# A depthwise dynamic convolution with routed experts: spread scoring, paired moves, and stores of 128 partitions

## The chip, the cores and the metric

The kernel runs on one core of a Trainium2 chip. The metric is the device time of one execution in microseconds; before the change it was measured three times. A core has five engines that run at once and wait for each other by semaphores: TensorE (PE in the profile; PEld is its weight load), VectorE (DVE), ScalarE (ACT), GpSimd (POOL) and SyncE (SP), which here only issues transfers. Sixteen DMA engines move data between HBM and the on-chip memory SBUF. Matmul results land in PSUM.

## The reference

Input x is 8 batches of 4,160 tokens with 192 channels. Each token has for each of 8 heads 7 weights, which go through a softmax over the 7 taps; the output of the first part is a causal convolution with these weights. The second part scores every token of that output, takes the best 128 of each batch, sends them through two layers of 1,024 hidden units, and adds the gated result.

```python
w = exp(weight_gen - max(weight_gen, -1)); w = w / (sum(w, -1) + 1e-9)     # [8, 4160, 8, 7]
x_pad = concatenate([zeros((8, 6, 192)), x], axis=1)
y[b, s, h] = sum over k of w[b, s, h, k] * x_pad[b, s + k, h]              # 24 channels per head
scores = y @ w_gate                                                        # [8, 4160]
for b in range(8):
    top = the 128 tokens of highest score
    ye = maximum(y[b, top] @ w1, 0) @ w2                                   # 192 -> 1024 -> 192
    out[b, top] = y[b, top] + sigmoid(scores[b, top])[:, None] * ye        # other rows: out = y
```

## The kernel before

The 33,280 tokens are cut into 128 runs of 260 consecutive tokens (SP = 260); partition p holds run p. The main loop takes 65 steps (NSUB) of C = 4 tokens on all partitions, and has one more round for the lag of the last step. The order of the instructions on each engine is the order in which the Python code issues them; there is no scheduler behind it. Each round g does the following, with the sums and the store one step behind the products.

- `products(g)` (L770): VectorE multiplies a sliding window of x (fp16, in the ring `xr` of 168 tokens) by the doubled weights `wd`, for 7 taps x 4 tokens x 192 channels. The result is a `prod` buffer, one of three. While no list of selected rows exists it is one instruction; afterwards it is two, of taps 0 to 3 and 4 to 6 (L783).
- `tap_sums(prod, cps, half)` (L789): TensorE adds up the taps by matmuls with blocks of a 64 x 64 identity, into the PSUM tile `cps`, one of two. The two halves of a round (`half` 0 and 1) take taps 0 to 3 and 4 to 6. Partition 64 j + p of `cps` holds, at index i, half j of the four tokens' channels (HB = 384 values) of run 64 i + p.
- `store(g, cps)` (L801): ScalarE copies `cps` into `co`, one of three fp32 buffers (`outp`), and SyncE issues two transfers, one for each j: 64 partitions, each with two rows of 384 values.

Beside that, generators are moved on by `advance` in each half: `sm` (softmax weights of later steps, L657), `dt` (dot products with the gate vector: transposes of x on TensorE, L712, evicted by ScalarE, L716, then small matmuls, L697; 50 groups), `sc` (scores, from weights and dot products, L720) and `sel`. How many `dt` moves a half gets is set by DOTS: 0.82 per half, so 1.64 per round. DOTS also sets the rounds in which the loads of tokens 168 to 259 are issued (`late`, L863).

`sel` begins when all scores exist. First comes `threshold_selection` (L435): five rounds of top-8 lists of each partition, four rounds of a search for the threshold with a matmul each, then a matmul chain of 40 that makes the list of rows. It takes nine moves, one per round. Then comes `expert_pass` (L202), which gathers the selected rows and their weights by indirect transfers of GpSimd, convolves them anew, and runs the experts' layers; it gets two moves per round. Its table `steps` (L397) says at which move after its start each of a batch's ten operations comes; a new batch begins every third move (EVERY). At the end `scatter_rows` (L411) writes the rows of the 8 batches over those of the convolution, by indirect transfers that wait for all stores.

Of the kernel before, what the change touches and what calls it, by code (L numbers as in the profile page):

```python
# [9 lines left out]
FP16 = mybir.dt.float16  # L10
# [10 lines left out]
def kernel(  # L21
# [10 lines left out]
    nc = tc.nc  # L32
    B, S, D = x.shape
    H, K = weight_gen.shape[2], weight_gen.shape[3]
# [4 lines left out]
    P = 128  # L39
    N = B * S  # L40
    SP = N // P
# [4 lines left out]
    C = 4  # L46
    NSUB = SP // C
    BIG = 58
    CH = C * H
    HB = C * D // 2  # L50
# [7 lines left out]
    MUL, ADD = ALU.mult, ALU.add  # L58
# [3 lines left out]
    out_flat = out.rearrange("b s d -> (b s) d")  # L62
# [139 lines left out]
    def expert_pass(rowf, gates, result, big):  # L202
# [3 lines left out]
            out=rown[:, :], in0=rowf, scalar1=float(N - 1), scalar2=0.0,  # L206
# [6 lines left out]
            out=wst[:, :], in0=rown[:, :], scalar1=float(-PAD), scalar2=0.0,  # L213
# [4 lines left out]
            out=win_i[:, :], in0=wst[:, :], scalar1=float(D), scalar2=None, op0=MUL,  # L218
# [3 lines left out]
            out=head[:, :], in0=rown[:, 0:1], scalar1=float(PAD), scalar2=1.0e6,  # L222
# [4 lines left out]
            out=head_i[:, :], in0=rown[:, 0:1], scalar=float(D), op0=MUL,  # L227
            in1=head[:, :], op1=ADD,
# [3 lines left out]
            out=pos[:, :], in0=rown[:, :], in1=boff[:, :], op=ALU.subtract  # L232
# [3 lines left out]
            out=posk[:, :, :], in0=pos[:, :, None].to_broadcast([P, B, K]),  # L236
            in1=koff[:, None, :].to_broadcast([P, B, K]), op=ADD,
# [3 lines left out]
            out=inside[:, :, :], in0=posk[:, :, :], scalar1=float(PAD), scalar2=None,  # L241
# [113 lines left out]
        def hidden(b, half):  # L355
            if half == 0:
                hTs[b] = moep.tile([P, FC, P], BF16, tag="hT", name="hT")
            hps = ps2.tile([P, FC // 2, P], FP32, tag="tps", name="hps")
            for j in range(FC // 2):
                f0 = (half * (FC // 2) + j) * P  # L360
                nc.tensor.matmul(  # L361
                    out=hps[:, j, :], lhsT=w1_a[:, f0:f0 + P], rhs=xeTs[b][:, 0, :],
                    start=True, stop=False,
                )
                nc.tensor.matmul(  # L365
                    out=hps[:, j, :], lhsT=w1_b[:, f0:f0 + P], rhs=xeTs[b][:, 1, :],
                    start=False, stop=True,
                )
            nc.scalar.activation(  # L369
                out=hTs[b][:, half * (FC // 2):(half + 1) * (FC // 2), :],  # L370
                in_=hps[:, :, :], func=AF.Relu,
            )
# [19 lines left out]
        def hand_over(b):  # L392
# [2 lines left out]
            result["ready"].append(b)  # L395

        steps = {  # L397
            0: row_weights, 2: scale_weights, 4: double, 6: tap_rows, 8: conv_rows,
            9: turn_rows, 10: lambda b: hidden(b, 0), 11: lambda b: hidden(b, 1),
            13: outputs, 14: hand_over,  # L400
        }
        for _ in range(GWAIT):
            yield
        for t in range(EVERY * (B - 1) + 15):
            for off in sorted(steps, reverse=True):
                b, rem = divmod(t - off, EVERY)
                if rem == 0 and 0 <= b < B:
                    steps[off](b)
            yield
# [23 lines left out]
    fast = {}  # L433
# [150 lines left out]
    def phase():  # L584
# [6 lines left out]
        prodp = cctx.enter_context(tc.tile_pool(name="prodp", bufs=3))  # L591
# [165 lines left out]
        state = {"scored": 0, "weights": 0, "exps": 0}  # L757
        wds = {}
# [8 lines left out]
            for j in range(b - a):  # L767
                wds[a + j] = wd[:, j]

        def products(s):  # L770
            o = s * C % RING
            wd = wds.pop(s)
            prod = prodp.tile([P, K, C, D], FP16, tag="prod", name="prod")
            xwin = bass.AP(
                tensor=xr.tensor, offset=xr[:, o:o + 1, 0:1].offset,
                ap=[list(xr[:, :, :].ap[0]), [D, K], [D, C], [G, H], [2, G // 2], [1, 2]],
            )
            pv = prod.rearrange("p k t (h a b) -> p k t h a b", h=H, b=2)
            wv = (
                wd.rearrange("p k (c h) b -> p k c h b", h=H)[:, :, :, :, None, :]  # L780
                .to_broadcast([P, K, C, H, G // 2, 2])
            )
            for k0, k1 in ((0, 4), (4, K)) if "rowf" in fast else ((0, K),):  # L783
                nc.vector.tensor_tensor(  # L784
                    out=pv[:, k0:k1], in0=xwin[:, k0:k1], in1=wv[:, k0:k1], op=MUL
                )
            return prod

        def tap_sums(prod, cps, half):  # L789
            pf = prod.rearrange("p k t d -> p k (t d)")  # L790
# [10 lines left out]
        def store(s, cps):  # L801
            co = outp.tile([P, 2, HB], FP32, tag="co", name="co")
            nc.scalar.copy(out=co[:, :, :], in_=cps[:, :, 0:HB])  # L803
            for j in range(2):
                nc.sync.dma_start(
                    out=bass.AP(
                        tensor=out_flat.tensor, offset=out_flat.offset + s * C * D + j * HB,
                        ap=[[SP * D, 64], [64 * SP * D, 2], [1, HB]],
                    ),
                    in_=co[64 * j:64 * j + 64, :, :],  # L810
                )

        def selected():
# [13 lines left out]
        for p0, p1 in ((1, Q), (Q, P)):  # L827
            nc.sync.dma_start(
                out=halo[p0:p1, :],
                in_=bass.AP(  # L830
                    tensor=x_flat.tensor, offset=x_flat.offset + (SP * p0 - PAD) * D,
                    ap=[[SP * D, p1 - p0], [1, PAD * D]],
                ),
# [10 lines left out]
            out=start_p[:, :], in_=identity.rearrange("p (b q) -> p b q", q=Q)[:, :, 0],  # L844
# [3 lines left out]
            out=keep_p[:, :], in0=start_p[:, :], scalar1=-1.0, scalar2=1.0, op0=MUL, op1=ADD  # L848
        )
        for n in range(2):  # L850
# [4 lines left out]
            if n == 0:  # L855
                nc.vector.tensor_scalar(
                    out=xflat[:, 0:PAD * D], in0=halo[:, :],
# [6 lines left out]
        for a in range(RING, SP, 20):  # L864
            b = min(SP, a + 20)
            free = (b - RING + PAD - 1) // C + 1
            late.append((max(free, int((a + PAD) / (2 * DOTS * RUN * GRP / D)) - 4), a, b))
        dt, sc, sel = dots(), score(), None
        dup_at = {a - 2: n for n, (a, b) in enumerate(pieces) if n > 1}

        def advance(gen):
            next(gen, None)

        prods = {}
        done_dots, groups = 0.0, 0
        for g in range(NSUB + 1):
            if g < NSUB:
                prods[g] = products(g)
            for half in range(2):
                if g < 2 or (half == 0 and state["exps"] <= max(g + 8, groups * 4 / 3 + 14)):  # L880
                    advance(sm)
                if g >= 1:
                    done_dots += DOTS
                    if done_dots >= 1:
                        done_dots -= 1
                        groups += 1
                        advance(dt)
                advance(sc)
                if sel is None:
                    if state["scored"] == NSUB and half == 0:  # L890
                        sel = selected()
                elif half == 1 or "rowf" in fast:
                    advance(sel)
                if half == 0:
                    if g in dup_at:
                        dup_weights(dup_at[g])
                    if g == RING // C - 10:
                        nc.scalar.copy(out=xr[:, 0:PAD, :], in_=xr[:, RING:RING + PAD, :])
                if g > 0:
                    if half == 0:  # L900
                        cps = ps_c.tile([P, 2, 512], FP32, tag="cps", name="cps")
                    tap_sums(prods[g - 1], cps, half)
            if g > 0:
                store(g - 1, cps)
            if late and g >= late[0][0]:
                load_x(*late.pop(0)[1:])
            if g == 5:
                selection_masks()
            if g == 10:
                selection_constants()  # L910
            if g == 34:
                expert_weights()
            if LOG:
                print(g, state, "rowf" in fast, "complete" in fast)
# [4 lines left out]
    LOG = False  # L919
    GWAIT = 4  # L920
    EVERY = 3
    DOTS = 0.82
    with ExitStack() as cctx:
        with tc.manual_schedule():
            phase()
    flag_v = nc.values_load(fast["flag"][0:1, 0:1], min_val=0, max_val=2 * P * B)
    with tc.If(flag_v > 0):
        with ExitStack() as fctx:
# [5 lines left out]
            for _ in expert_pass(fast["rowf"][:, :], zero, undo, big):  # L934
                pass
# [5 lines left out]
                out=sv[:, :],  # L941
                in_=bass.AP(tensor=s_d.tensor, offset=s_d[:, :].offset, ap=[[S, B], [1, S]]),
# [3 lines left out]
            for i in range(CAP // 8):  # L946
# [4 lines left out]
                    out=sv[:, :], in_to_replace=top_v[:, sl], in_values=sv[:, :],  # L951
# [10 lines left out]
                out=sc_t[:, :], in_=bass.AP(tensor=v_d.tensor, offset=v_d[:, :].offset, ap=swap)  # L962
            )
            nc.sync.dma_start(
                out=ix_t[:, :], in_=bass.AP(tensor=i_d.tensor, offset=i_d[:, :].offset, ap=swap)
# [4 lines left out]
                out=row_g[:, :], in0=row_g[:, :], in1=boff[:, :], op=ADD  # L970
            )
            for _ in expert_pass(row_g[:, :], gate_values(sc_t[:, :]), redo, big):
                pass
# [36 lines left out]
```

## Time and profile before

| | |
|---|---|
| time, median of three | 321.94 us (320.14 to 322.54) |
| span of the profiled execution | 319.0 us |
| busy: TensorE / VectorE / ScalarE / GpSimd | 198.0 / 249.3 / 188.5 / 70.5 us |
| stores of the output | 130, of 192 KB each |
| HBM read and written | 41.60 and 26.35 MB |

The page divides the span into 40 slices of 8 us. Each digit is the busy share of an engine in tenths; the last two rows are the granted TensorE clock in tenths of full speed and the mean busy share of the sixteen DMA engines.

```
PE   0287298759688495999646414456617788799100
DVE  3786676988876396999999999999979988897000
ACT  4699579998955799699643203123305576766100
PEclk9999769986969788799989555556765979999755
DMA  6979999899999789946646302312739976355420
```

Read by columns: up to slice 19 (150 us) scoring and softmax run beside the convolution, and all engines and the DMA engines are busy. In slices 19 to 27 VectorE alone is full, with the threshold search. From slice 30 the experts run. In the last two or three slices the rows are scattered. A busy share is an average over its slice and does not say which engine others wait for; that takes the lists of waits and the chain.

### The profile page before, as it was taken

How to read it: one execution, taken by the hardware profiler on the slowest of the kernel's cores; microseconds unless marked ns; L12 is line 12 of the kernel's file. 1: busy time of each engine (PE TensorE's matmuls, PEld its weight loads, DVE VectorE, ACT ScalarE, POOL GpSimd, SP SyncE). 2: the span in 40 equal slices, each digit the busy share in tenths (PEclk: the TensorE clock that was granted, in tenths of full speed). 3: DMA queues.
4: the chain of work that ended last, by engine and by line, in shares of the span. 5: the costliest groups of instructions: out<-in, count | busy, mean ns of one | idle time of the engine just before them, and what ended most of it. 6: DMA issues, size and time to landing. Idle time of an engine off the chain costs nothing.

```text
span 319.0 us, 7498 instructions
## 1 busy us (share of the span) xinstructions
PE 198.0 (62%) x3177; PEld 124.3 (39%) x3177; DVE 249.3 (78%) x248; ACT 188.5 (59%) x282; POOL 70.5 (22%) x94
## 2 busy tenths in 40 slices
PE   0287298759688495999646414456617788799100
PEld 0155165536455263666323201114304455566000
DVE  3786676988876396999999999999979988897000
ACT  4699579998955799699643203123305576766100
POOL 2891020130120004000000000002388760000180
PEclk9999769986969788799989555556765979999755
DMA  6979999899999789946646302312739976355420
GB/s 162 301 173 249 296 235 222 184 240 254 273 234 241 261 161 215 208 117 150 170 128 150 95 7 59 89 49 63 185 60 163 203 179 148 78 120 129 106 84 16
DMA packets 28080, 51.48 MB, mean 161 GB/s; under 512 B 4805, under 2 KB 22219, under 8 KB 28042
## 3 DMA queue, kind: packets, MB, share of 16 engines
q1 hardware_dynamic: 21962, 33.62, 35.8%
q0 software_dynamic: 6080, 17.34, 30.8%
q8 instruction: 26, 0.43, 0.5%
q14 instruction: 12, 0.10, 0.1%
HBM read 41.60 MB, written 26.35 MB: 213 GB/s over the span
## 4 chain that ended last, share of the span: by engine, by line
PE 28%; ACT 23%; DVE 21%; DMA 13%; issue 8%; POOL 3%; SPq 1%; POOLq 0%; ACTq 0%; DVEq 0%
DVE prod L784 13%; PE cps L795 13%; DMA out_dram<-co 10%; ACT e L635 6%; ACT co L803 5%; ACT xT L716 4%; PE tps L712 4%; ACT wd L763 3%; POOL out_dram L417 2%; PE den L189 2%; PE yps L697 2%; PE yep L377 2%; DMA wg_t<-in_weight_gen_dram 2%; PE aps L335 1%; PE hps L361 1%
## 5 line engine op out<-in xcount | busy, mean ns | idle before, releaser
L784 DVE TENSOR_TENSOR prod<-xr,wd 128x5376 f16<-128x5376 f16 (+1 forms) x83 | 192.4, 2345 | 10.9 <-PE cps L795 5.4
L795 PE MATMUL cps<-prod,ident 64*64 64x384 f16 x1820 | 117.0, 386 | 26.7 <-DVE prod L784 22.9
L803 ACT COPY co<-cps 128x768 f32<-128x768 f32 x65 | 52.9, 814 | 63.2 <-PE cps L795 43.9
L795 PEld LDWEIGHTS <-ident 64*64 64x64 f16 x1820 | 49.8, 121 | 74.8 <-DVE prod L784 30.6
L716 ACT COPY xT<-tps 128x1024 f16<-128x1024 f16 (+1 forms) x50 | 50.7, 1026 | 4.8 <-PE tps L712 4.8
L712 PE MATMUL tps<-ident,xr 128*128 128x128 f16 x399 | 35.3, 240 | 0.0
L249 POOL DMA_INDIRECT wsel<-in_weight_gen_dram,row_i x8 | 13.1, 1638 | 96.0 <-DVE win_i L217 93.9
L697 PE MATMUL yps<-gmat,xT 128*128 128x8 f16 (+1 forms) x399 | 17.9, 169 | 22.5 <-ACT y L702 18.3
L635 ACT ACTIVATE e<-wg_t 128x896 f16<-128x896 f32 (+2 forms) x18 | 29.9, 1662 | 3.1 <-DMA wg_t<-in_weight_gen_dram 3.1
L697 PEld LDWEIGHTS <-xT 128*128 128x128 f16 x399 | 14.2, 98 | 37.1 <-issue 24.2
L763 ACT COPY wd<-w 128x1792 f16<-128x1792 f16 (+2 forms) x18 | 27.9, 1551 | 0.8 <-DVE w L651 0.8
L712 PEld LDWEIGHTS <-xr 128*128 128x128 f16 x399 | 26.6, 107 | 0.6 <-issue 0.6
L189 PEld LDWEIGHTS <-ident 128*128 128x128 f16 x182 | 11.0, 107 | 39.4 <-issue 34.8
L628 POOL COPY tick<-e 1x1 f16<-1x1 f16 x13 | 9.7, 747 | 58.5 <-ACT e L635 58.5
L189 PE MATMUL den<-e,ident 128*128 128x128 f16 (+2 forms) x126 | 11.1, 238 | 15.7 <-ACT e L635 14.6
L734 DVE TENSOR_TENSOR sp<-w,y 128x1792 f16<-128x1792 f16 (+2 forms) x9 | 9.0, 1000 | 14.0 <-ACT y L702 14.0
L601 POOL DMA_DIRECT2D xr<-in_x_dram x20 | 10.9, 548 | 34.4 <-DVE prod L784 33.3
L417 POOL DMA_INDIRECT out_dram<-xr,row_i x8 | 7.8, 980 | 39.7 <-issue 39.7
L369 ACT ACTIVATE hT<-hps 128x512 bf16<-128x512 f32 x16 | 9.6, 601 | 9.9 <-PE hps L365 8.0
L189 PE MATMUL den<-es,ident 128*128 128x8 f16 x56 | 2.6, 167 | 16.3 <-ACT es L297 16.3
L271 POOL DMA_INDIRECT xr<-in_x_dram,win_i x8 | 11.2, 1400 | 5.6 <-DVE xr L320 3.8
L651 DVE TENSOR_TENSOR w<-e,r 128x896 f16<-128x896 f16 (+2 forms) x18 | 10.3, 573 | 2.2 <-ACT r L199 2.1
(127 smaller groups left out, 182.0 us busy)
## 6 DMA issues: line engine op xcount, KB each, us to landing
out_dram<-co SPq DMA_DIRECT2D x130, 192.0 KB, 3.1
wg_t<-in_weight_gen_dram SPq DMA_DIRECT2D x15, 448.0 KB, 3.9
xr<-in_x_dram POOLq DMA_DIRECT2D x6, 672.0 KB, 7.8
xr<-in_x_dram POOLq DMA_DIRECT2D x4, 960.0 KB, 13.6
xr<-in_x_dram POOLq DMA_DIRECT2D x4, 480.0 KB
xr<-in_x_dram POOLq DMA_DIRECT2D x3, 576.0 KB
xr<-in_x_dram POOLq DMA_DIRECT2D x2, 384.0 KB
halo<-in_x_dram SPq DMA_DIRECT2D x1, 504.0 KB, 5.3
```

The lines of the kernel that those rows point to most:

```text
L189: nc.tensor.matmul(out=den[:, :, :], lhsT=ident16[:, :], rhs=e_k(k), start=(k == 0), stop=(k == K - 1),)
L249: nc.gpsimd.indirect_dma_start(out=wsel[:, b, :], out_offset=None, in_=wg_flat[:, :], in_offset=bass.IndirectOffsetOnAxis(ap=row_i[:, b:b ...
L271: nc.gpsimd.indirect_dma_start(out=win_of(b), out_offset=None, in_=x_elems, in_offset=bass.IndirectOffsetOnAxis(ap=win_i[:, b:b + 1], axis=0),
L417: ins = nc.gpsimd.indirect_dma_start(out=out_flat[:, :], out_offset=bass.IndirectOffsetOnAxis(ap=result["at"][:, b:b + 1], axis=0), in_=re ...
L635: nc.scalar.activation(out=es[n][:, :, :, :], in_=wgts[n].rearrange("p (s c) h k -> p s k (c h)", c=C), func=AF.Exp)
L697: nc.tensor.matmul(out=o, lhsT=lhs, rhs=m, start=(w == 0), stop=(w == 2), skip_group_check=True,)
L712: nc.tensor.transpose(out=tps[:, j, :], in_=xflat[:, e0:e0 + RUN], identity=ident16[:, :],)
L716: nc.scalar.copy(out=xT[:, 0:m, :], in_=tps[:, 0:m, :])
L763: nc.scalar.copy(out=wd[:, 0:b - a, :, :, :], in_=w16[:, a:b, :, :, None].to_broadcast([P, b - a, K, CH, 2]),)
L784: nc.vector.tensor_tensor(out=pv[:, k0:k1], in0=xwin[:, k0:k1], in1=wv[:, k0:k1], op=MUL)
L795: nc.tensor.matmul(out=cps[64 * j:64 * j + 64, i, 0:HB], lhsT=ident16[rows, rows], rhs=pf[rows, k, j * HB:(j + 1) * HB], start=(k == 0), s ...
L803: nc.scalar.copy(out=co[:, :, :], in_=cps[:, :, 0:HB])
```

## The change

Four edits come together. Spread scoring: DOTS goes from 0.82 to 0.66, so that the 50 groups of dot products take 40 rounds instead of 32 and scoring ends in round 45; the late loads of x are issued later to suit. Selection and experts in paired moves: `sel` moves on in both halves of every round from its start, and the table `steps` of the experts is packed from 15 to 10 moves per batch. Products in two parts: once `sel` exists, a round's product is issued as two instructions, one ahead of each half's moves, so that moves stand between them on VectorE. Stores of 128 partitions: the two transfers of a step are now taken by i instead of j. Each reads one row of 384 values from all 128 partitions, and writes the four tokens of 64 runs; its pattern in HBM is two halves, 64 runs, 384 values.

```diff
         steps = {
-            0: row_weights, 2: scale_weights, 4: double, 6: tap_rows, 8: conv_rows,
-            9: turn_rows, 10: lambda b: hidden(b, 0), 11: lambda b: hidden(b, 1),
-            13: outputs, 14: hand_over,
+            0: row_weights, 1: scale_weights, 2: double, 3: tap_rows, 4: conv_rows,
+            5: turn_rows, 6: lambda b: hidden(b, 0), 7: lambda b: hidden(b, 1),
+            8: outputs, 9: hand_over,
         }
         for _ in range(GWAIT):
             yield
-        for t in range(EVERY * (B - 1) + 15):
+        for t in range(EVERY * (B - 1) + 10):
...
-        def products(s):
+        def products(s, prod, k0, k1):
             o = s * C % RING
-            wd = wds.pop(s)
-            prod = prodp.tile([P, K, C, D], FP16, tag="prod", name="prod")
+            wd = wds[s]
...
-            for k0, k1 in ((0, 4), (4, K)) if "rowf" in fast else ((0, K),):
-                nc.vector.tensor_tensor(
-                    out=pv[:, k0:k1], in0=xwin[:, k0:k1], in1=wv[:, k0:k1], op=MUL
-                )
-            return prod
+            nc.vector.tensor_tensor(
+                out=pv[:, k0:k1], in0=xwin[:, k0:k1], in1=wv[:, k0:k1], op=MUL
+            )
...
             nc.scalar.copy(out=co[:, :, :], in_=cps[:, :, 0:HB])
-            for j in range(2):
+            for i in range(2):
                 nc.sync.dma_start(
                     out=bass.AP(
-                        tensor=out_flat.tensor, offset=out_flat.offset + s * C * D + j * HB,
-                        ap=[[SP * D, 64], [64 * SP * D, 2], [1, HB]],
+                        tensor=out_flat.tensor,
+                        offset=out_flat.offset + (64 * i * SP + s * C) * D,
+                        ap=[[HB, 2], [SP * D, 64], [1, HB]],
                     ),
-                    in_=co[64 * j:64 * j + 64, :, :],
+                    in_=co[:, i, :],
                 )
...
         for g in range(NSUB + 1):
+            split = sel is not None
             if g < NSUB:
-                prods[g] = products(g)
+                prods[g] = prodp.tile([P, K, C, D], FP16, tag="prod", name="prod")
             for half in range(2):
+                if g < NSUB:
+                    if split:
+                        products(g, prods[g], *((0, 4), (4, K))[half])
+                    elif half == 0:
+                        products(g, prods[g], 0, K)
...
                 if sel is None:
-                    if state["scored"] == NSUB and half == 0:
+                    if state["scored"] == NSUB and half == 1:
                         sel = selected()
-                elif half == 1 or "rowf" in fast:
+                else:
                     advance(sel)
...
-    DOTS = 0.82
+    DOTS = 0.66
```

## The prediction, made before the changed kernel ran

> **What bounds the kernel now.** I read the page's engine shares first, then the stages, because the shares (VectorE 78%, ScalarE 59%, TensorE 62%) belong to stages with different limits. The answer of the trace by stretches (busy us of each engine, its count of instructions, granted TensorE clock, DMA share, GB/s):
>
> ```profile
> 20.00:150.00 130.00, 101.54 (x1743) 66.97 (x1746) 101.87 (x68) 110.73 (x140) 20.37 (x44) 0.86 0.92 221
> 150.00:185.00 35.00, 19.42 (x328) 10.29 (x321) 34.66 (x40) 15.65 (x19) 0.00 (x0) 0.82 0.51 130
> 185.00:215.00 30.00, 12.36 (x130) 4.52 (x129) 28.99 (x44) 5.59 (x6) 0.00 (x0) 0.50 0.21 53
> 215.00:240.00 25.00, 12.27 (x204) 7.32 (x208) 22.06 (x34) 6.59 (x14) 12.24 (x7) 0.70 0.45 103
> 240.00:298.00 58.00, 47.04 (x726) 31.24 (x715) 49.37 (x54) 37.67 (x85) 17.19 (x11) 0.91 0.67 146
> ```
>
> From 20 to 150 us, while scoring runs beside the convolution, no compute engine is full (VectorE 101.87 of 130), but the DMA engines are at 0.92. From 150 to 222 us VectorE alone is full: one product of 2.95 us per step plus the selection. From 240 us the experts run and VectorE is at 49.37 of 58. What ends last is the stores, then the scatter of the rows:
>
> ```profile
> 23.20:300.50 277.30, 189.43 (x3076) 118.50 (x3073) 234.96 (x236) 173.02 (x260) 46.59 (x55) 0.81 0.70 165
> 300.50:319.00 18.50, 0.00 (x0) 0.00 (x0) 0.00 (x0) 0.00 (x0) 8.40 (x15) 0.50 0.13 44
> ```
>
> The first store is issued at 23.2, the last lands at 300.5, and 18.5 us of scatter and end follow. The transfers, from the page's DMA parts (queue; then issues with KB each and us to landing) and from the waits:
>
> ```profile
> q1 hardware_dynamic: 21962, 33.62, 35.8%
> q0 software_dynamic: 6080, 17.34, 30.8%
> ...
> out_dram<-co SPq DMA_DIRECT2D x130, 192.0 KB, 3.1
> ...
> ACT co L803 <- PE cps L795: 43.9, 20, 10.0
> ...
> ACT co L803 <- DMA out_dram<-co: 11.3, 3, 5.1
> ```
>
> The reader is to see that 130 stores land in 3.1 us each, that ScalarE's eviction into `co` waits far more for TensorE's sums (43.9 us) than for a store to give back its buffer (three times, 11.3 us), and that all queues together use 35.8 + 30.8, about 67%, of sixteen DMA engines. A kernel that has 67% on sixteen engines has no room for running half its bytes on two.
>
> [...]the 6-row store of `zpad` (L173) left seven updates of its semaphore in the trace's update records, one of the sequencer and then six, while the loads and stores with 128 or 64 rows outermost leave sixteen. No run yet shows a pattern whose two sides differ. [...]1,536-byte packets of the stores take 65 ns when alone and about 107 ns when the sixteen engines are all on one store of 64 partitions (between 199 and 200 us).
>
> **The change part by part.**
>
> *Stores.* Before, each of a step's two stores is out [64 rows][2][384] from 64 partitions: outermost 64 on both sides[...]. After, the out side is [2][64 rows][384] from 128 partitions; the built program carries it so: 2 outermost in DRAM, 128 in SBUF. [...]All 130 stores then go through the same two DMA engines, 64 packets of 1,536 bytes on each instead of 8. The packet records of before hold 16,640 such packets (130 x 128); they follow each other every 61 ns on one engine in an unbroken run at 200.0 us, and a packet takes 62 ns at least, 65 in the median, 85 in the mean. [...]I take 62 ns: 8,320 packets x 62 ns = 516 us on each of the two. The ends: [...]the median of 65 gives 541 us.
>
> *What else those two engines carry.* Loads of x, weights and gathers keep sixteen engines, so each engine keeps its share. Outside of the stores the packet records sum to 104 us per engine after 23.2 us. With each size at its uncontended median it is about 80. I take 92. It adds to the 516[...].
>
> *Sum.* First store at 23.2 (nothing before it changes: same loads, same first products) + 516 + 92 + the tail of 18.5 (the scatters wait for every store and keep their form) = 650 us of span; the time was 3 us over the span before (321.9 against 319.0), so about 652. I say 650. Per step of the last third, without loads, it is 2 x 64 x 62 ns = 7.9 us, against 4.3 before (277.3 us / 65 steps).
>
> *Who waits for it.* `outp` has three buffers, so the eviction of step g waits for the stores of step g-3. Behind that eviction ScalarE holds everything queued after it: transposes' evictions (L716), exponentials, doubled weights (L763), the experts' copies. TensorE then waits for `cps` buffers (two), VectorE for `prod` (three). With six stores in flight the two engines never run dry, so nothing hides their 608 us and all the rest hides beside them. x loads share the two engines but run up to eight steps ahead, some 70 us at the new pace.
>
> *Scoring over 42 steps (DOTS 0.82 to 0.66).* The same 50 groups at 1.32 instead of 1.64 per step; the last scored piece is at step 45 instead of 37, late x loads at steps 20 to 32 instead of 15 to 25. No instruction is added. It would thin out the stretch with 0.92 DMA share, where VectorE idles 28 us; beside two full DMA engines it is worth nothing.
>
> *Two moves per step, products in two parts.* Selection takes 9 half-steps instead of 9 steps, so it ends its list at step 50 (46 before) although it begins 7.5 steps later. The forms of before's VectorE rows:
>
> ```profile
> L784 DVE TENSOR_TENSOR prod<-xr,wd 128x5376 f16<-128x5376 f16 x47 | 138.2, 2952 | 10.2 <-PE cps L795 4.7 <-ACT wd L763 4.1 <-issue 1.2
> L784 DVE TENSOR_TENSOR prod<-xr,wd 128x3072 f16<-128x3072 f16 x18 | 31.5, 1753 | 0.7 <-PE cps L795 0.7
> L784 DVE TENSOR_TENSOR prod<-xr,wd 128x2304 f16<-128x2304 f16 x18 | 24.3, 1352 | 0.0
> ```
>
> Split steps go from 18 to 19: 1753 + 1352 - 2952 = 153 ns once. Hidden.
>
> *Experts' chain, 10 moves instead of 15 per batch.* No operation is added; each hand-over has half a step instead of one. At 4 us per half-step of the new pace, the slowest hand-over seen (wait of `es` for its gathered weights, 7.7 us, once) hardly matters. Five moves instead of three are left after the last step; 5 x about 1 us lies beside the last three steps' stores (24 us). Nothing.
>
> **The rivals.**
>
> *A: the stores still use sixteen engines, and the schedule gains.* For it: the trace shows no pattern with unequal outermost sizes[...]. Against: [...]six updates on six rows. Then VectorE decides: 249.3 busy + 7.7 idle before 20 us + 11.5 idle between 222 and 298 + 21 after 298 = 289.5, plus half of the 28 us that it idles from 20 to 150 = 303.5 span, about 306 us: faster.
>
> *B: sixteen engines, but the pace of the moves costs more than the spreading gains.* For it: only half a product (1.35 to 1.75 us) covers a round trip over TensorE; the 40 matmuls of the picked list took 2.9 us from `place` to `got`, and VectorE waited 6.1 us for `yep` in eight batches already. Eight batches with 1.5 us more, and 1 us in the list, is 13 us; if the early stretch stays bound by transfers, 322 + 13 = 335: slower, by far less.
>
> *C: two engines per store, but other ones each time.* Then 12 of 16 engines can be busy with six stores in flight; a store takes 64 x 62 ns + 2, about 6 us, which three buffers hide: about 318, within or just over 1%.[...]
>
> **How the numbers follow.** Two engines for all stores: 0.85. A: 0.09. B: 0.03. C: 0.03, on the border. The predicted time is that of the first, 650. Its bounds:[...] 23 + 541 + 104 + 18.5 + 3 = 690 at the highest[...]. I trim the low end[...] and give 590 to 715; what is left out is A to C and a little of the first, below 2 in 10. Faster by over 1%: 0.10, within 1%: 0.02, slower: 0.88.
>
> **What would show it.** Right: the median of stores to landing rises from 3.1 to about 20 us; "ACT co <- DMA out_dram<-co" becomes the largest wait, hundreds of us; the chain is mostly DMA out_dram<-co; the mean DMA share falls below 0.45 though every byte is the same; VectorE near 39% of the span, evenly low, with no full stretch; store packets back at 62 to 65 ns. Wrong: a landing of 3 us with VectorE at 80% or more is A, waits of `we` and `yep` grown over 10 us with it is B. If stores land in about 6 us and the DMA share stays at 0.6 or above, it is C.

## The result, and the profile after

The changed kernel takes 643.68 us (median of four runs, 642.55 to 645.11) against 321.04 us before in the same session: a ratio of 2.005, 95% interval 1.993 to 2.017. It is twice as slow. Here and below a time is the median of all runs of a kernel, and a ratio compares its faster runs with those of the kernel before, so that the quotient of two times can differ from the ratio. The page of the profiled execution, first the busy time of the engines, then the DMA share by slices of 16 us, the two large queues, and the chain of work that ended last, by line:

```profile
PE 250.1 (39%) x3177; PEld 156.0 (24%) x3177; DVE 252.7 (39%) x249; ACT 189.4 (29%) x282; POOL 67.3 (10%) x94
...
DMA  8834333224428762111111111111252132111111
...
q0 software_dynamic: 6080, 17.34, 15.0%
q1 hardware_dynamic: 20142, 33.61, 14.6%
...
DMA out_dram<-co 63%; SPq L802 22%; ACT co L800 3%; ACT xT L716 1%; ACT e L635 1%; POOL out_dram L417 1%; DMA wg_t<-in_weight_gen_dram 1%; PE cps L792 1%; PE den L189 1%; ACT wd L763 0%; ACT lnd L197 0%; PE aps L335 0%; ACT r L199 0%; PE sps L741 0%; ACT hT L369 0%
```

VectorE and ScalarE work as many microseconds as before (252.7 and 189.4 against 249.3 and 188.5), so no work was added; the bytes are the same too (33.61 MB on q1). TensorE's sum rose from 198.0 to 250.1 us with a lower granted clock (0.62 instead of 0.80), but it is at 39% of the span. What the reader is to see is the row of ones: in about half of the slices the mean share of sixteen DMA engines is a little over a tenth, and yet 85% of the chain are stores, landing (63%) or being issued (22%). A stretch without loads, by time (same columns as before):

```profile
300.00:450.00 150.00, 65.09 (x801) 38.39 (x794) 79.06 (x89) 37.59 (x47) 0.00 (x0) 0.60 0.14 51
```

No engine is over 53% here, and the DMA share is 0.14. Two full engines of sixteen would be 0.125. The waits (us in total, times, longest) tell how the stores reach the engines:

```profile
ACT co L800 <- DMA out_dram<-co: 373.2, 60, 23.7
...
PE cps L792 <- ACT co L800: 127.3, 26, 19.2
...
DVE prod L782 <- ACT wd L763: 58.8, 9, 11.8
```

ScalarE's eviction waits for a `co` buffer in 60 of 65 steps, 373.2 us instead of 11.3; TensorE waits behind it for `cps`, and VectorE for what stands behind it on ScalarE, such as the doubled weights.

Two kinds of records in the trace say the rest. The packet records carry no engine number, but their times are enough: between 500 and 502 us the 1,536-byte packets of the stores form two interleaved rows, each with a packet every 61 ns, and there are no others. A store is issued every 3.9 us and takes about 15 us to land, so several are in flight at once, and all of them are on the same pair of engines. The update records tell how often the semaphore of a transfer was raised. 122 of the 130 new stores left exactly three updates; of the stores before, 110 left sixteen. (The others have updates of neighbours mixed in, or lack some.) Read as the prediction reads the 6-row store, one update is SyncE's and two are of engines; for a store issued at 331.03 us the first came at 335.21, when the issue ended, and the other two at 345.37 and 345.65.

### The profile page after: what moved, and what is told of

It reads as the page before. It is cut to its first block, busy times and chain, and to the rows that moved or that the text cites. A ratio compares the mean times of both kernels' runs of the same rounds, so it can differ in the third digit from the quotient of the medians.

```text
span 642.4 us, 7486 instructions
## 1 busy us (share of the span) xinstructions
PE 250.1 (39%) x3177; PEld 156.0 (24%) x3177; DVE 252.7 (39%) x249; ACT 189.4 (29%) x282; POOL 67.3 (10%) x94
## 3 DMA queue, kind: packets, MB, share of 16 engines
q1 hardware_dynamic: 20142, 33.61, 14.6%
## 4 chain that ended last, share of the span: by engine, by line
DMA 64%; SPq 22%; ACT 8%; PE 2%; POOL 1%; issue 1%; ACTq 0%; DVE 0%; POOLq 0%
DMA out_dram<-co 63%; SPq L802 22%; ACT co L800 3%; ACT xT L716 1%; ACT e L635 1%; POOL out_dram L417 1%; DMA wg_t<-in_weight_gen_dram 1%; PE cps L792 1%; PE den L189 1%; ACT wd L763 0%; ACT lnd L197 0%; PE aps L335 0%; ACT r L199 0%; PE sps L741 0%; ACT hT L369 0%
## 5 line engine op out<-in xcount | busy, mean ns | idle before, releaser
L792 PE MATMUL cps<-prod,ident 64*64 64x384 f16 x1820 | 142.4, 455 | 127.3 <-ACT co L800 127.3
L800 ACT COPY co<-cps 128x768 f32<-128x768 f32 x65 | 51.9, 799 | 378.8 <-DMA out_dram<-co 373.2
L792 PEld LDWEIGHTS <-ident 64*64 64x64 f16 x1820 | 64.7, 140 | 183.8 <-issue 156.9
L712 PE MATMUL tps<-ident,xr 128*128 128x128 f16 x399 | 43.3, 276 | 0.0
L189 PEld LDWEIGHTS <-ident 128*128 128x128 f16 x182 | 12.1, 114 | 93.6 <-issue 90.6
L249 POOL DMA_INDIRECT wsel<-in_weight_gen_dram,row_i x8 | 8.8, 1101 | 235.0 <-DVE win_i L217 232.8
L712 PEld LDWEIGHTS <-xr 128*128 128x128 f16 x399 | 33.1, 125 | 0.6 <-issue 0.6
L741 PE MATMUL sps<-sp,ident 128*128 128x256 f16 (+2 forms) x63 | 12.9, 378 | 41.8 <-ACT lnd L197 41.8
L628 POOL COPY tick<-e 1x1 f16<-1x1 f16 x13 | 10.1, 776 | 163.2 <-ACT e L635 163.2
L752 DVE TENSOR_REDUCE scores<-ss 128x32 f32<-128x256 f32 (+2 forms) x9 | 3.5, 393 | 48.3 <-ACT ss L746 48.3
L741 PEld LDWEIGHTS <-ident 128*128 128x128 f16 x63 | 7.7, 133 | 46.0 <-issue 44.1
L271 POOL DMA_INDIRECT xr<-in_x_dram,win_i x8 | 13.6, 1703 | 50.3 <-DVE xr L320 49.1
```

The lines of the kernel that those rows point to most:

```text
L189: nc.tensor.matmul(out=den[:, :, :], lhsT=ident16[:, :], rhs=e_k(k), start=(k == 0), stop=(k == K - 1),)
L271: nc.gpsimd.indirect_dma_start(out=win_of(b), out_offset=None, in_=x_elems, in_offset=bass.IndirectOffsetOnAxis(ap=win_i[:, b:b + 1], axis=0),
L712: nc.tensor.transpose(out=tps[:, j, :], in_=xflat[:, e0:e0 + RUN], identity=ident16[:, :],)
L741: nc.tensor.matmul(out=sps[:, :, :], lhsT=ident16[:, :], rhs=sp[:, :, k, :], start=(k == 0), stop=(k == K - 1),)
L792: nc.tensor.matmul(out=cps[64 * j:64 * j + 64, i, 0:HB], lhsT=ident16[rows, rows], rhs=pf[rows, k, j * HB:(j + 1) * HB], start=(k == 0), s ...
```

## The experiments

The base is the kernel before or the kernel after, as the text of each says. Experiments 1 to 4 are single runs, and their effects are ten times as large as the spread of the runs or more. All times stand against runs of the kernel before in the same session (319.08, 318.69 and 319.78 us).

**1. The new stores alone, in the kernel before.**

```diff
-            for j in range(2):
+            for i in range(2):
...
-                        ap=[[SP * D, 64], [64 * SP * D, 2], [1, HB]],
+                        ap=[[HB, 2], [SP * D, 64], [1, HB]],
...
-                    in_=co[64 * j:64 * j + 64, :, :],
+                    in_=co[:, i, :],
```

> The kernel before with the new stores alone. Theory (130 stores on two DMA engines set the time): 8,320 packets x 61 ns on each of the two, about 84 us of other packets on them, 29 us ahead of the first store packet, 19 us tail: 640 us, within 15 us of the changed kernel, whatever the schedule is. Rival (the paired moves and the thinner scoring are part of the loss): clearly below, 500 us or less.

Measured: 641.84 us (one run). Its wait:

```profile
ACT co L803 <- DMA out_dram<-co: 376.7, 60, 17.9
```

This is the changed kernel's time and wait without any of the schedule edits. The new stores alone give the whole loss.

**2. The stores of before, cut so that two engines get them.** Each 64-row store of the kernel before becomes one of 62 rows and one of 2 rows; the pattern, with the row dimension outermost on both sides, stays.

```diff
             for j in range(2):
-                nc.sync.dma_start(
+                for r0, r1 in ((0, 62), (62, 64)):
+                    nc.sync.dma_start(
...
-                    in_=co[64 * j:64 * j + 64, :, :],
+                        in_=co[64 * j + r0:64 * j + r1, :, :],
```

> The kernel before, each of its stores (64 rows outermost on both sides, pattern unchanged) cut into one of 62 rows and one of 2 rows. Theory[...]: again 64 packets per engine and store on two engines, about 640 us. Rival (it is the unequal outermost sizes, 2 in HBM against 128 in SBUF, or the 128 partitions, that slow the new stores): no such pattern here, so about 322 us, a little more for twice as many issues.

Measured: 642.70 us (one run). Issues (KB each) and wait:

```profile
out_dram<-co SPq DMA_DIRECT2D x130, 186.0 KB
...
out_dram<-co SPq DMA_DIRECT2D x130, 6.0 KB
...
ACT co L803 <- DMA out_dram<-co: 379.4, 59, 18.4
```

The same bytes go to the same rows in packets of the same size as before, and the kernel is as slow as with the new pattern. So it is neither the 128 partitions nor that the two sides differ. The time is that of 128 packets per step on each of two engines, as the expectation has it; the time alone shows the two engines here. A cut into two stores that both keep sixteen engines was not run, so the price of 260 issues instead of 130 is not known by itself; the next experiment, with as many issues, limits it.

**3. The same cut at 51 and 13 rows,** whose largest divisors are 3 and 13.

> The kernel before, each of its stores cut into one of 51 rows (largest divisor 3) and one of 13 rows (13). Theory: the three fullest engines get 2 x (34 + 2) = 72 packets per step, 65 x 72 x 61 ns = 286 us, with 84 us of other packets, 29 ahead and 19 behind: about 420 us (405 to 440). Rival (a store on few engines is slow for another reason than its packets per engine, such as a fixed cost for each store): no more than 340 us, or as slow as with two engines.

Measured: 423.65 us (one run), 4 us from the expectation.

```profile
out_dram<-co SPq DMA_DIRECT2D x130, 153.0 KB
...
out_dram<-co SPq DMA_DIRECT2D x130, 39.0 KB
...
ACT co L803 <- DMA out_dram<-co: 138.6, 40, 12.0
```

The time follows the number of packets on the fullest engine, 128 per step at 642 us and 72 at 424. That is 56 packets in each of 65 steps, 3,640 in all, for 218 us: 60 ns each, about the spacing of 61 ns in the packet records. The records of this run show the counts too: 119 of the 130 stores of 51 rows leave four updates of their semaphore, and 119 of the 130 of 13 rows fourteen, so three and thirteen engines. Between 200 and 280 us three store packets are under way at once for most of the time.

**4. The new stores issued by GpSimd,** in the changed kernel: `nc.sync` becomes `nc.gpsimd` in `store`.

> The changed kernel, its stores issued by GpSimd instead of SyncE. Theory (a pattern with 2 outermost goes to two engines[...]): with six stores in flight most engines work, so the time falls far below 644 us; a store takes 64 x 62 ns and its landing, 6 us, GpSimd issues 130 more transfers[...]: 330 to 400 us. Rival (the pattern itself is slow, or the pair is fixed here too): 600 us or more.

Measured: 387.28 us (one run).

```profile
q0 software_dynamic: 53920, 43.37, 55.9%
...
out_dram<-co POOLq DMA_DIRECT2D x130, 192.0 KB, 11.0
```

The question is whether the pair of engines stays the same on another path. It does not seem to: between 300 and 340 us four of the stores' packets are most often under way at once, where the changed kernel had two. (The 55.9% of queue q0 hold the loads of GpSimd too, which it moved before as well.) Each store comes as 42 packets of 4,608 and two of 1,536 bytes, as two shares of 64 rows would make. The time lies inside the expectation, but its working does not hold: a store lands in 11.0 us, not 6, and there are 38,220 records of 12 bytes that the other runs don't have. So the result fits a pair that changes from store to store, and excludes that the pattern is slow whoever issues it. As the path and the packets change with the issuing engine, the pair alone was not tested, and why a store takes 11 us was not looked into.

**5. The schedule edits alone: the changed kernel with the stores of before.**

> The changed kernel with the stores of before. Theory: the schedule edits cost nothing, and without the stores' two engines VectorE decides again: about 306 us, up to 3% below the 334 of no gain at all. Rival (the faster pace of the moves makes waits): 325 to 335 us, with waits of we, yep and es grown by over 10 us in sum.

Measured: 330.67 us, a ratio of 1.038 (1.031 to 1.046). The theory fell: the schedule edits do not gain 5%, they lose 4%. The next three split them. Experiments 6 and 8 lose 1.9 and 1.4%, together about this loss.

**6. Paired moves, packed table and two-part products alone:** stores of before, DOTS 0.82, and one more `scatter_rows(fast)` behind the loop, since the experts now end inside it.

> The changed kernel with the stores of before and DOTS back at 0.82; the rows are scattered after the loop, since the experts end inside it. So paired moves, packed table and two-part products alone. Theory M (the old-store version's loss of 3.8% lies in the spread scoring: a burst of late loads of x, and a selection that begins 8 steps later and leaves five moves behind the last step): no loss here, 312 to 322 us, and the stretch from the last product to the end is shorter by 2 us or more. Rival N (the doubled pace of the moves costs waits on TensorE and ScalarE hand-overs): 326 us or more.

Measured: 326.32 us, a ratio of 1.019 (1.011 to 1.026). Theory M expected no loss here; it fell as well. VectorE's waits from 147 to 300 us:

```profile
DVE xr L320 <- ACT wes L314: 6.6, 7, 1.0
...
DVE xr L385 <- PE yep L377: 1.3, 2, 1.0
```

In seven of eight batches VectorE stands about 0.9 us ahead of the rows' product, until ScalarE has doubled the weights. In the kernel before, from 147 to 298 us, this wait came once; there the product of a whole half-step stood between:

```profile
DVE xr L320 <- ACT wes L314: 0.9, 1, 0.9
```

**7. The same with the table of before,** 15 moves per batch (only `steps` and the `+ 15` go back).

> The kernel with the stores of before, DOTS 0.82 and paired moves, but with the experts' table of before, 15 moves per batch. Theory P (the packed table costs: VectorE waits 6.6 us in seven batches for ScalarE's doubled weights one half-step earlier): the loss of 1.9% of the packed version mostly goes, 317 to 322 us, and the wait of the rows' product for the doubled weights falls below 2 us. Rival Q (the loss is in the paired selection and in splitting more products): 324 us or more.

Measured: 316.04 us, a ratio of 0.995 (0.990 to 0.999). So the packed table was the loss; the paired selection with its two-part products costs nothing, and a gain of half a per cent is hardly clear of the noise. Of VectorE's waits from 147 to 300 us only this is left:

```profile
DVE xr L385 <- PE yep L377: 2.9, 3, 1.5
```

The wait for the doubled weights, 6.6 us, is most of the 7.6 us between the two profiled spans (322.8 and 315.2 us).

**8. Spread scoring alone,** DOTS 0.66 in the kernel before.

> The kernel before with DOTS 0.66 alone. The selection then begins in round 45 at one move per round, and 17 moves of the experts' pass are left behind the last product. Theory M: the burst of late loads as in the old-store version, plus some 17 x 1.3 us of moves with nothing beside them: 340 to 350 us. Rival N: the spread alone gains, and the moves left over are worth less than that: 325 us or less.

Measured: 322.87 us, a ratio of 1.014 (1.007 to 1.022). The time lies in rival N's range, but its account does not hold: the spread alone gains nothing, it loses 1.4%. The 17 moves left over cost less than theory M had. The last product ends 7 us sooner (285.4 against 292.8 us), and the stretch behind it is 11 us longer (36.9 against 26.2 us): the moves lie beside the last stores and the first scatters, but the last three scatters wait for the experts, 6.3 us in all. The burst is there. (A ticket is a one-element copy on GpSimd, L628, of a softmax exponential; a load that stands behind it can't start before that exponential is done.) GpSimd's timeline (start, duration, instruction, in brackets the idle time ahead):

```profile
98.75 2.97 POOL L628 COPY tick<-e 1x1 f16<-1x1 f16 x1 [17.37 <-ACT e L635]
101.66 2.66 POOL L601 DMA_DIRECT2D xr<-in_x_dram  x5
```

The last ticket is delayed with the slower softmax, the late loads wait behind it in GpSimd's order, and five loads start within 3 us. Then stores starve. The kernel before from 20 to 90 and from 90 to 150 us, then this one:

```profile
20.00:90.00 70.00, 52.44 (x900) 34.59 (x899) 54.44 (x41) 62.13 (x77) 16.12 (x36) 0.86 0.98 240
90.00:150.00 60.00, 49.10 (x847) 32.39 (x847) 47.43 (x27) 48.59 (x64) 4.25 (x8) 0.85 0.85 199
```

```profile
20.00:90.00 70.00, 54.76 (x968) 36.28 (x968) 61.53 (x43) 58.75 (x72) 35.13 (x29) 0.90 0.97 238
90.00:150.00 60.00, 34.34 (x546) 21.81 (x545) 35.80 (x20) 39.90 (x50) 9.30 (x13) 0.73 0.84 196
...
ACT co L803 <- DMA out_dram<-co: 27.7, 4, 11.6
```

The last line is the wait of ScalarE for a store to give back its buffer, 11.3 us before. VectorE works 35.80 of the second 60 us, in the kernel before 47.43. All that was gained up to 90 us (61.53 against 54.44) is given back: step 30 ends at 148.0 us, before at 147.7.

**9. An earlier softmax, so that no ticket is late:** experiment 5 with a gate of 5/3 instead of 4/3 groups. (The gate says how far the softmax may run ahead of the groups of dot products.)

> The changed kernel with the stores of before, and the softmax of later steps moved on as early as before (5/3 instead of 4/3 groups in its gate), so that the ticket of the last paced load is not held up on GpSimd and the late loads of x queued behind it don't start all at once. Theory M1 (the burst starves the stores and holds ScalarE for 17 us): that wait is gone, step 31 is reached at 145 us or sooner instead of 156, and the whole takes 317 to 323 us. Rival M2 (the loads need the same DMA time whenever they come; the burst only moves the wait): 328 to 333 us.

Measured: 330.27 us, a ratio of 1.037 (1.031 to 1.043); step 30 ends at 147.3 us. M2 had the time right. Step 30 ends when it ended in the kernel before (147.7), though a fifth less scoring is done by then. The loads had moved forward again, still in a burst (four start at 88.2 us). M2's reason, that the loads need the same time whenever they come, is not shown by this; experiment 11 shows that it matters when they come.

**10. Scoring over fewer steps, with paired moves:** experiment 5 with DOTS 0.74, a gate of 1.48 groups, and the scatter behind the loop.

> Stores of before, paired moves, DOTS 0.74 with the softmax's gate at 1.48 groups, the rows scattered after the loop: scoring ends 4 steps earlier than with 0.66, so that all experts' moves lie beside products. Theory M: neither a burst nor moves left over; 308 to 318 us, faster than before by 1 to 3%. Rival N: 324 us or more.

Measured: 325.10 us, a ratio of 1.015 (1.008 to 1.021). A miss: no moves are left over, but the packed table and the unpaced loads are in it. What each of them costs here was not separated.

**11. Spread scoring with its loads spread too:** experiment 8, and four of the late loads each behind the ticket of a later exponential.

```diff
             if n in paced:
                 after_exp(n)
                 load_x(*paced[n])
+            if n in paced_late:
+                after_exp(n)
+                load_x(*paced_late[n])
...
+        paced_late.update({14 + k: late[k][1:] for k in range(4)})
+        late = late[4:]
```

> The kernel before with DOTS 0.66, and four of the five late loads of x each behind a ticket of a later exponential (pieces 14 to 17), so that they come about 9 us apart instead of in a burst. Theory L (all schedules reach step 30 at 147 to 152 us because all loads are drawn in by then and the DMA engines are full; loads moved behind step 30 free some 10 us there): step 30 at 143 us or sooner, 315 to 319 us in all, 1 to 2% below the version with DOTS 0.66 alone. Rival K (pacing only delays scoring, and the early stretch is held by the order of ScalarE and TensorE work): step 30 at 147 us or later, 322 us or more.

Measured: 309.77 us, a ratio of 0.978 (0.972 to 0.983), against 1.014 in experiment 8; step 30 ends at 128.8 us. GpSimd's late loads now, and the stretch from 90 to 150 us:

```profile
103.23 0.53 POOL L601 DMA_DIRECT2D xr<-in_x_dram  x1 [0.22 <-DVE prod L787]
...
111.16 0.53 POOL L601 DMA_DIRECT2D xr<-in_x_dram  x1 [0.31 <-issue]
...
119.40 0.53 POOL L601 DMA_DIRECT2D xr<-in_x_dram  x1 [0.70 <-DVE scores L755]
...
128.76 1.06 POOL L601 DMA_DIRECT2D xr<-in_x_dram  x2
```

```profile
90.00:150.00 60.00, 49.92 (x876) 32.61 (x869) 53.64 (x29) 53.18 (x68) 10.90 (x17) 0.88 1.02 235
```

Stores and loads alternate, VectorE works 53.64 of 60 us, and the wait for stores is down from 27.7 to 7.6 us. Theory L has the direction and the place, but it forecast too little: step 30 comes at 128.8 us instead of 143, and the whole takes 310 us instead of 315 to 319. Rival K is excluded.

**12. The same with DOTS 0.74.**

> The same with DOTS 0.74: the loads come one step closer to each other and the selection begins 4 steps sooner. Theory L: 312 to 318 us. Rival K: 321 us or more.

Measured: 306.34 us, a ratio of 0.950 (0.942 to 0.959). This is the fastest kernel of the study, 4% (by the medians) to 5% below the kernel before and less than half of the changed one; theory L had 312 to 318 us. Its runs lie between 300 and 314 us. Paced loads together with the paired moves and the wide table of experiment 7 were not run.

## Why the prediction was right, and where it was not

- **Two engines for all stores: right, and shown.** The new stores alone give the whole loss (1), stores of 62 and 2 rows give the same time (2), stores of 51 and 13 rows the time computed for three engines (3), and the update records count two, three and thirteen engines. Rival C, a pair that changes, is excluded by the two rows of packets while several stores are in flight; on GpSimd's path the records fit it (4).
- **516 us of store packets: about right.** They follow each other every 61 ns: 8,320 x 61 = 508 us. A packet takes 65 ns in the mean, instead of 85 in the kernel before; that holds for the 62-row stores of experiment 2 as well. That it would take 62 was the author's estimate, and why packets are shorter here was not shown. (The median in the kernel before is 68 ns over all 16,640 packets; the 65 of the prediction is that of a packet alone.)
- **92 us of other packets: about right.** The first store packet starts at 29.1 us and the last at 623.5; 594 minus 508 leaves 86. That is a remainder; the records of the other packets in this stretch sum to 97 us per engine, if the sixteen share them evenly.
- **The rest of the sum.** 29.1 + 508 + 86 + 18.9 behind the last packet = 642 us of span; as 86 is a remainder, this sum can't fail. Against the prediction's 650 the store packets are 8 us less and the others 6 us less, and the 6 us from the first issue to its first packet were not in it. That the total came within 1% is in part these errors taking each other away.
- **Who waits: right, with two signs off.** ScalarE waits 373.2 us, 60 times; a step without loads takes 7.8 us (7.9 predicted); VectorE is at 39% as forecast. The landing was put at about 20 us; the page gives none for these stores, but the last update comes 15 us after the start of the issue in the median. VectorE is not evenly low: from 434 to 466 us, with the selection, it is full.
- **Schedule edits at nothing: right only beside the two engines.** Experiment 1 and the changed kernel differ by less than 2 us. By themselves the edits lose 3.8%, and there rival A's 306 us was wrong by 25. The step of rival A that failed is "half of the 28 us that it idles from 20 to 150": spreading the dot products does not spread the loads, which run ahead of them in GpSimd's order, so the early stretch kept its length (9) until the loads were paced (11). Rival B had the right sign and nearly the time (335), in part by luck: of the loss, the faster moves are 1.9%, with the wait at another place (the doubled weights, not `yep` or the list; 6, 7), and the spread scoring, from which B expected nothing, is 1.4% (8). The packed expert chain costed at "nothing" is about 2% where no store hides it.

What was not shown: why a store is given 2, 3, 13 or 16 engines. That the new stores would get two, and all of them the same two, was the author's estimate ahead of the run. The runs show the counts, and that the pair stays, not how it is picked.

## What to carry to other kernels

Look at the outermost dimension of both sides of a transfer before anything else. By the update records a store of 64 rows went to sixteen engines, one of 51 rows to three, one of 13 to thirteen, the 6-row transfer to six, and one with 2 outermost in HBM against 128 partitions to two; stores of 62 and 2 rows took the time of two. So what counted in these was not how many partitions a store touches: each count is the largest number up to 16 that divides both outermost sizes. That is read off these forms alone. The time then followed the packets on the fullest engine, 61 ns for each of 1,536 bytes. A mean DMA share of 0.14 beside a chain full of DMA meant two full engines here, not idle ones. And spreading compute over more steps spreads nothing if the loads come in a burst all the same; spread scoring lost 1.4% with its loads in a burst and gained 2.2% with the loads paced.

## What the runs showed of the hardware that was not expected

- SyncE itself was held by the stores on two engines. The issue of one took 3.8 us in the median instead of 0.6, about the 64 x 61 ns that a store needs on its engine; it is 22% of the chain. The kernel before, then the changed one:

```profile
L805 SPq DMA_DIRECT2D out_dram<-co x130: 595/599/1832, 23.2 to 297.1; - x130
```

```profile
L802 SPq DMA_DIRECT2D out_dram<-co x130: 511/3808/17240, 23.0 to 609.0; - x130
```

A load of weights that followed two of these stores in the same queue, at 50.20 us, took 3.72 us to issue; one that followed another transfer, at 124.11 us, took 0.54.
- A one-element copy on GpSimd, the ticket, took from 0.18 to 13.41 us in the kernel of experiment 11, and 9.48 us once in that of experiment 5. In the kernel before, nine of the 13 copies took 0.18 us. The other four (2.91, 2.40, 0.69 and 2.12 us) each began while a VectorE product of 2.95 us ran and ended within 0.06 us after a VectorE instruction: three after the product, one after the instruction that followed it. So a copy could last longer than the product beside it; 13.41 us is more than four products. What held the copies was not shown. No run took the products away.
